# A fused attention and feed-forward kernel: the attention steps of two batches in another order, with empty steps, and a padded fifth chunk of keys

## The chip, the cores and the metric

The kernel runs on one core of a Trainium2 chip. The metric is the device time of one execution in microseconds; three runs of the kernel before gave a median of 1037.28 us (1033.76 to 1042.06).

## The reference

Causal attention over 4 batches of 8 heads, 576 positions and 64 columns per head, with a bias from running sums of `s`, then two feed-forward networks over the 2304 tokens:

```python
scores = scale * q @ k.T                    # per batch and head, 576 x 576
cum = cumsum(maximum(s, 0)); bias = -(cum[:, None] - cum[None, :])
scores = where(causal, -1e9, scores + minimum(bias, 0))
attn = softmax(scores) @ v                  # heads side by side: x is 2304 x 512
x = ((x @ w_a) * (x @ w_b)) @ w_out         # 512 -> 1536 -> 512
h = x @ w_in                                # 512 -> 2048
out = (maximum(h, 0) + alpha * minimum(h, 0)) @ w_out2   # 2048 -> 512
```

The weights arrive as 64-bit floats and are decoded on the chip.

## The kernel before

The tokens are cut into five blocks, four of 512 and one of 256. For each block `ffn` runs both networks. Every product is made of three TensorE multiplications of 512 columns (L997 to L999, L1106 to L1108): operands are split into a high and a low part (`xh`, `xl`, `wh`, `wl`, `gh`, `gl`), and low times low is left out. The weights are decoded in the first block, kept in memory as `w_d`, and loaded again as `raw` for each further block.

A batch has 576 rows, so its attention is done in two pieces: rows 0 to 511, four row blocks of 128 (r = 0 to 3), and the last 64 rows (r = 4), for which two heads share one tile. Attention of block 0's rows runs first, alone. The rest is cut into steps that stand between the multiplications of `ffn`: while the network of block n runs, the attention that block n + 1 needs is done, for rows 0 to 511 of batch a = n + 1 and the last 64 rows of batch b = n. There are four pairs of heads (i = 0 to 3), and for each pair these steps:

- `loads`: keys and queries (`kq`), values (`vb`), running sums (`cb`). `kq` has three buffers, `vb` four.
- `both` and `biases`: bias and causal mask of one or two row blocks are written to tiles `z`. `z` of r = 4 has one buffer.
- `s01`, `s23`, `s4`: scores of r = 0 and 1, of r = 2 or 3, and of r = 4 (L472, L647) go into two PSUM banks, which all attention steps share. `soften` then makes the probabilities: minimum, exponential, sum and scaling on VectorE, ScalarE and GpSimd.
- `turn`, `t4`: the probabilities are transposed by TensorE. Only batches below `TURN` = 2 do it so. From there on (`turned`) VectorE transposes within 32 x 32 squares into `zt`, which goes through memory (`zd<-zt`, then `pt<-zd` for r = 0 to 3 or `pb<-zd` for r = 4) to bring the squares into place. `pb` has one buffer, which `av_b` gives back.
- `two_av`: `av_b` (L766, or L774 in batches below `TURN`), then `av` (L707 or L714), probabilities times values; both wait until their probabilities are in place.

The function `attention` lists the steps of one block. Its first few (`lead`) are put among the steps of the block before, six from that list's end. The loop at the end of the kernel spreads the list over the `ffn`: a step is run when its share of 1 / 1.06 of the network's groups of three multiplications is reached, so the steps are evenly spaced, whatever they hold.

Nothing is ordered by the hardware or a compiler. While the program is written, the class `Order` keeps a clock for each engine and places VectorE's, ScalarE's, GpSimd's and SP's instructions by due times and by its own costs; `run.need` places what a step must have behind it. Each engine then serves its instructions strictly in the order placed. All loads and stores go through SP's one queue.

Of the kernel before, what the change touches and what calls it, by code (L numbers as in the profile page):

```python
# [18 lines left out]
P = 128  # L19
D = 64  # L20
# [33 lines left out]

SUMS_PE = 2

TURN = 2


FROM_WEIGHTS, AHEAD, FROM_LEAD, FROM_STEPS, STEPS = 2, 10, 3, 4, 3  # L60
# [132 lines left out]
def attention_two_moe_kernel(  # L193
# [10 lines left out]
    nc = tc.nc  # L204
# [8 lines left out]
    QA = 4 * P  # L213
    QB = S - QA
# [32 lines left out]
    SEEN = 100  # L247
# [28 lines left out]
    def scale(o, i, s0, s1):  # L276
        n = size(o)
        eng = yield Either(pool=115 + 1.09 * n, dve2=70 + 0.52 * n), SEEN
        (nc.gpsimd if eng == "pool" else nc.vector).tensor_scalar(
            o, i, s0, s1, op0=ALU.mult, op1=ALU.mult  # L280
        )

    def dma(o, i):
        yield {"sp": 480}, 700
        nc.sync.dma_start(o, i)
        yield {"dma": prod(o.shape) / 90}, 900
# [84 lines left out]
    pb_t, scores = {}, []  # L371
# [5 lines left out]
    def slot():  # L377

        ring.append(ring.pop(0))
        if ring[-1] in reader:  # L380
            run.need(reader[ring[-1]])
        return ring[-1]

    def read_by(i, gen):
        reader[i] = run.spawn(gen)
        return reader[i]

    def load_v(b, hp, u):
        c0 = 2 * hp * D
        got = []  # L390

        def chain():
            yield of_vb
            vr = raw.tile([P, 5, 2 * D], F32, name="vb", tag="vb", bufs=VB)
            got.append(vr)
            if b + u >= TURN:
                keys = v[b, 0:QA, c0:c0 + 2 * D].rearrange("(c j k) d -> j k c d", j=4, k=32)
                if u:
                    yield {"pool": 240}, SEEN
                    nc.gpsimd.memset(vr[:, 4, :], 0.0)  # L400
                for j in range(4):
                    yield from dma(vr[j::4, 0:4, :], keys[j])
                    if u and j < 2:
                        k0 = QA + 32 * j
                        yield from dma(vr[j::4, 4, :], v[b, k0:k0 + 32, c0:c0 + 2 * D])
                return
            yield from dma(
                vr[:, 0:4, :], v[b, 0:QA, c0:c0 + 2 * D].rearrange("(c p) d -> p c d", p=P)
            )
            if u:  # L410
                yield from dma(vr[0:QB, 4, :], v[b, QA:S, c0:c0 + 2 * D])

        v_t[b, hp, u] = got, run.spawn(chain(), slack=SL_QK)
# [72 lines left out]
    def biases(b, h, rs):  # L486
# [10 lines left out]
        def chain():  # L497
# [5 lines left out]
            c = 0  # L503
            if r == 4 and b + 1 >= TURN:
                yield {"pool": 180}, SEEN
# [40 lines left out]
    def turned(b, h, rs, z):  # L546

        yield of_zt
        n = z.shape[1] // P
        zt = work.tile([P, 4 * n * 32], F32, name="zt", tag="zt", bufs=ZT)  # L550
        zd = dram.tile([4, P, n * 32], F32, name="zd", tag=f"zd{n}", bufs=8)
        yield from dve(
            n * P, 1.04, nc.vector.transpose, zt.rearrange("p (j t n) -> p j t n", j=4, n=32),
            z.rearrange("p (t j n) -> p j t n", j=4, n=32),
        )
        run.give(of_z[rs[0]], run.t)
        yield from dma(
            zd.rearrange("i (k j) m -> (i k) (j m)", j=4), zt
        )
        run.give(of_zt, run.t)  # L560
        if rs[0] == 4:
            yield of_pb
            pb_t[h] = raw.tile([P, 5 * P], F32, name="pb", tag="pb")
            o = pb_t[h].rearrange("p (i m) -> p i m", i=4)
        else:
            s0 = rs[0] * (rs[0] + 1) // 2 * 32
            o = pts[h % 4].rearrange("p (i m) -> p i m", i=4)[:, :, s0:s0 + n * 32]
        yield from dma(o, zd.rearrange("i p m -> p i m"))

    def soften(b, h, rs, srcs, *banks_read):  # L570
# [14 lines left out]
        def rest():  # L585
# [10 lines left out]
            for i, p in enumerate(parts):  # L596
                yield from scale(p, p, sm[:, i:i + 1], 1.0)
            if b + (rs[0] == 4) >= TURN:
                e_t[b, h, rs[0]] = run.spawn(turned(b, h, rs, z), run.t)
# [54 lines left out]
    def probabilities(b, h, r):  # L654
        first = z_t[b, h, r][1]
        run.need(first)
        z, rest = z_t.pop((b, h, r))
        run.need(rest)
        return z
# [32 lines left out]
    def av(b, hp, blk):  # L692

        turned = b >= TURN
        if turned:
# [30 lines left out]
    def t4(b, hp, j):  # L726

        if j == 0:
            z_t[b, hp, 4] = probabilities(b, hp, 4)
        z = z_t[b, hp, 4]  # L730
        k, n = (QB, P) if j else (P, QA)
        at = slot()
        tp = banks[at][0:k, 0:n]
        for c in range(n // P):
            k0 = j * QA + c * P
            nc.tensor.transpose(tp[:, c * P:(c + 1) * P], z[:, k0:k0 + k], ident)
        run.pe(n / P * 107)
        if j:
            z_t.pop((b, hp, 4))
            run.give(of_z[4])  # L740

        def chain():
            if j == 0:
                yield of_pb
                pb_t[hp] = raw.tile([P, 5 * P], F32, name="pb", tag="pb")
            o = j * QA
            yield from copy(pb_t[hp][0:k, o:o + n], tp, 1.04)

        e_t[b, hp, 4 + j] = read_by(at, chain())

    def av_b(b, hp, blk):

        turned = b + 1 >= TURN
        if turned:
            settle((b, hp, 4))
        else:
            run.need(*(e_t.pop((b, hp, 4 + j)) for j in range(2)))
        got, ready = v_t.pop((b, hp, 1))
        run.need(ready)
        pb = pb_t.pop(hp)  # L760
        at = slot()
        pv = banks[at][:, 0:QB]
        for c in range(5 if turned else 0):
            for j in range(2):
                p = pb.rearrange("p (i t n) -> p i t n", i=4, n=32)
                nc.tensor.matmul(  # L766
                    pv[64 * j:64 * j + 64], got[0][:, c, j * D:(j + 1) * D],
                    p[:, 2 * j:2 * j + 2, c, :], start=c == 0, stop=c == 4,
                )
        for c in range(0 if turned else 5):  # L770
            for j in range(2):
                k = QB if c == 4 else P
                o = c * P + j * QB
                nc.tensor.matmul(  # L774
                    pv[64 * j:64 * j + 64], got[0][0:k, c, j * D:(j + 1) * D], pb[0:k, o:o + QB],
                    start=c == 0, stop=c == 4,
                )
        run.pe(5 * 107)
        run.give(of_vb)
        run.give(of_pb)  # L780
        x_done[blk].append(read_by(at, finish(pv, b * S + QA, QB, hp, blk)))
# [6 lines left out]
    HP = H // 2  # L788
# [46 lines left out]
    def attention(blk):  # L835

        b, a = blk - 1, blk
        has_a = a < B
        steps = []

        def add(f, pair, *args):
            if 0 <= pair < HP:
                steps.append((f, args))

        def loads(i):
            if has_a:
                load_kq(a, i, 0)
                if a >= SUMS_PE:
                    for j in range(2):
                        load_sums(a, 2 * i + j, 0)  # L850
                load_v(a, i, 0)
            load_kq(b, i, 1)
            load_sums(b, i, 1)
            load_v(b, i, 1)

        lead = [(loads, (0,))]
        if has_a:
            lead.append((both, (a, 0, (0, 1))))
        for i in range(HP + 1):
            j = i - 1  # L860

            def turns(c):
                for k in range(2 if a < TURN else 0):
                    add(turn, j, a, 2 * j + k, c)

            def last(p, k):
                if blk < TURN:
                    add(t4, p, b, p, k)

            if has_a:  # L870
                add(s01, i, a, i)
                add(both, i, a, i, (2,))
                turns(0)
                add(both, i, a, i, (3,))
                add(s23, i, a, i, 2)
                last(j, 0)
                turns(1)
                last(j, 1)
                add(s23, i, a, i, 3)
                add(biases, i, b, i, (4,))  # L880
                add(loads, i + 1, i + 1)
                turns(2)
                add(both, i + 1, a, i + 1, (0, 1))
                add(two_av, j, a, b, j, blk)
                add(s4, i, b, i)
            else:
                add(biases, i, b, i, (4,))
                add(loads, i + 1, i + 1)
                add(s4, i, b, i)
                last(i, 0)  # L890
                last(i, 1)
                add(av_b, i - (blk >= TURN), b, i - (blk >= TURN), blk)
        return lead, steps
# [230 lines left out]
    for blk in range(NB):  # L1124
# [5 lines left out]
        steps = plan[blk][1]  # L1130
# [76 lines left out]
```

## Time and profile before

| | before |
|---|---|
| median of three runs | 1037.28 us |
| profiled execution | 1038.65 us |
| its span on the core | 1036.9 us |
| TensorE busy | 1004.5 us (97%) |
| VectorE busy | 712.4 us (69%) |
| ScalarE busy | 541.7 us (52%) |
| GpSimd busy | 214.9 us (21%) |
| mean granted TensorE clock | 0.990 |

Times are microseconds from the start of the span. PE is TensorE, DVE VectorE, ACT ScalarE, POOL GpSimd, SPq SP's issue of a DMA. The attention that runs alone ends at about 56 us; the five network blocks end at about 287, 515, 740, 935 and 1035 us. A granted clock of 1.00 is the upper level (2.4 GHz), 0.50 the lower (1.2 GHz); a mean between them says that a stretch had both. A matmul's duration includes its way through the array, so neighbours overlap; pace is read from the starts.

### The profile page before, as it was taken

How to read it: one execution, taken by the hardware profiler on the slowest of the kernel's cores; microseconds unless marked ns; L12 is line 12 of the kernel's file. 1: busy time of each engine (PE TensorE's matmuls, PEld its weight loads, DVE VectorE, ACT ScalarE, POOL GpSimd, SP SyncE). 2: the span in 40 equal slices, each digit the busy share in tenths (PEclk: the TensorE clock that was granted, in tenths of full speed). 3: DMA queues.
4: the chain of work that ended last, by engine and by line, in shares of the span. 5: the costliest groups of instructions: out<-in, count | busy, mean ns of one | idle time of the engine just before them, and what ended most of it. 6: DMA issues, size and time to landing. Idle time of an engine off the chain costs nothing.

```text
span 1036.9 us, 16084 instructions
## 1 busy us (share of the span) xinstructions
PE 1004.5 (97%) x5385; PEld 807.2 (78%) x5385; DVE 712.4 (69%) x1693; ACT 541.7 (52%) x1124; POOL 214.9 (21%) x279
## 2 busy tenths in 40 slices
PE   6999999999999999999799999997999999999998
PEld 5577787777677787877678787876888888889997
DVE  6998998998866657677366859674444465545685
ACT  5876666666653446444254435452433344446564
POOL 2131211211111224232021214241100012210032
PEclk9999999999999999999899999998999999999999
DMA  7687968567857674875267575765335524227551
GB/s 199 192 268 258 296 236 287 177 211 249 275 169 195 203 206 153 225 194 183 71 201 227 176 209 174 191 193 164 127 99 164 175 70 147 95 74 250 184 178 39
DMA packets 128866, 191.53 MB, mean 185 GB/s; under 512 B 26576, under 2 KB 62416, under 8 KB 128784
## 3 DMA queue, kind: packets, MB, share of 16 engines
q1 hardware_dynamic: 128784, 190.51, 59.6%
q8 instruction: 42, 0.69, 0.3%
q14 instruction: 40, 0.33, 0.1%
HBM read 153.44 MB, written 37.04 MB: 184 GB/s over the span
## 4 chain that ended last, share of the span: by engine, by line
PE 70%; DMA 2%; DVE 1%; issue 1%; ACT 1%; SPq 0%; ACTq 0%; DVEq 0%
PE bank L997 16%; PE bank L998 16%; PE bank L999 16%; PE bank L1106 5%; PE bank L1107 5%; PE bank L1108 5%; PE bank L472 2%; PE bank L707 2%; DMA kq<-in_kq_a_dram 1%; PE bank L766 1%; PE bank L647 1%; ACT z L254 0%; DMA pb<-zd 0%; DVE wl L274 0%; DMA vb<-in_v_dram 0%
## 5 line engine op out<-in xcount | busy, mean ns | idle before, releaser
L997 PE MATMUL bank<-xh,wh 128*128 128x512 f32 (+1 forms) x800 | 303.5, 379 | 1.3 <-ACT wh L262 1.1
L999 PE MATMUL bank<-xh,wl 128*128 128x512 f32 (+1 forms) x800 | 296.0, 370 | 1.3 <-POOL wl L274 1.3
L998 PE MATMUL bank<-xl,wh 128*128 128x512 f32 (+1 forms) x800 | 295.5, 369 | 0.0
L262 ACT ACTIVATE wh<-raw 128x512 fp32r<-128x512 f32 x265 | 165.9, 627 | 113.0 <-PE bank L998 63.8
L274 DVE TENSOR_TENSOR wl<-raw,wh 128x512 fp32r<-128x512 f32 x200 | 139.6, 699 | 112.4 <-ACT wh L262 107.6
L997 PEld LDWEIGHTS bank<-xh,wh 128*128 128x128 f32 x800 | 151.2, 189 | 42.9 <-issue 13.4
L999 PEld LDWEIGHTS bank<-xh,wl 128*128 128x128 f32 x800 | 151.3, 189 | 28.2 <-POOL wl L274 2.2
L998 PEld LDWEIGHTS bank<-xl,wh 128*128 128x128 f32 x800 | 151.5, 189 | 24.3
L274 POOL TENSOR_TENSOR wl<-raw,wh 128x512 fp32r<-128x512 f32 x72 | 94.1, 1307 | 322.8 <-ACT wh L262 288.9
L262 ACT ACTIVATE gh<-g 128x512 fp32r<-128x512 f32 (+1 forms) x140 | 82.2, 587 | 66.3 <-DVE g L268 57.7
L274 DVE TENSOR_TENSOR gl<-g,gh 128x512 fp32r<-128x512 f32 (+1 forms) x125 | 87.9, 704 | 41.3 <-ACT gh L262 39.1
L1106 PE MATMUL bank<-wh,gh 128*128 128x512 f32 x288 | 115.3, 401 | 0.4 <-ACT wh L262 0.4
L1107 PE MATMUL bank<-wl,gh 128*128 128x512 f32 x288 | 112.6, 391 | 0.2 <-DVE wl L274 0.2
L1108 PE MATMUL bank<-wh,gl 128*128 128x512 f32 x288 | 112.4, 390 | 0.0
L254 ACT ACTIVATE z<-z,mn 128x128 f32<-128x128 f32 (+4 forms) x144 | 83.0, 579 | 49.5 <-DVE mn L268 49.4
L268 DVE SCALAR_TENSOR_TENSOR w<-raw,w 128x512 int32<-128x512 int32 x136 | 92.5, 699 | 0.1
L997 PE MATMUL bank<-gh,wh 128*128 128x512 f32 (+1 forms) x240 | 90.4, 377 | 0.0
L998 PE MATMUL bank<-gl,wh 128*128 128x512 f32 (+1 forms) x240 | 88.7, 369 | 0.3 <-DVE gl L274 0.2
L999 PE MATMUL bank<-gh,wl 128*128 128x512 f32 (+1 forms) x240 | 88.6, 369 | 0.0
L254 ACT ACTIVATE m<-bank 128x512 f32<-128x512 f32 (+1 forms) x80 | 44.1, 551 | 69.8 <-PE bank L999 69.6
L262 ACT ACTIVATE a_sb<-bank 128x512 f32<-128x512 f32 (+1 forms) x60 | 33.1, 552 | 76.6 <-PE bank L999 75.7
L1106 PEld LDWEIGHTS bank<-wh,gh 128*128 128x128 f32 x288 | 54.2, 188 | 13.8 <-issue 2.5
(83 smaller groups left out, 1321.8 us busy)
## 6 DMA issues: line engine op xcount, KB each, us to landing
raw<-w_d SPq DMA_DIRECT2D x136, 512.0 KB, 4.4
raw<-in_w_dram SPq DMA_DIRECT2D x68, 512.0 KB, 4.6
w_d<-w SPq DMA_DIRECT2D x68, 256.0 KB, 3.1
kq<-in_kq_a_dram SPq DMA_DIRECT2D x32, 256.0 KB, 5.7
zd<-zt SPq DMA_DIRECT2D x32, 192.0 KB, 1.9
pt<-zd SPq DMA_DIRECT2D x32, 192.0 KB, 2.9
kq<-in_kq_b_dram SPq DMA_DIRECT2D x16, 352.0 KB, 7.0
vb<-in_v_dram SPq DMA_DIRECT2D x80, 64.0 KB, 3.9
```

Of the source, the lines that this page charges most:

```text
L254: nc.scalar.activation(o, i, func, **k)
L262: nc.scalar.activation(o, i, AF.Copy)
L268: f(*args, **k)
L274: (nc.gpsimd if eng == "pool" else nc.vector).tensor_tensor(o, i0, i1, op=ALU.subtract)
L472: nc.tensor.matmul(dst[j], got[0][o, QA + r * P:QA + n], got[0][o, 0:n], start=b >= SUMS_PE, stop=True)
L707: nc.tensor.matmul(pv[64 * j:64 * j + 64, r * P:(r + 1) * P], got[0][:, c, j * D:(j + 1) * D], p[:, :, r * (r + 1) // 2 + c, :], start=c = ...
L997: nc.tensor.matmul(o, wh, ih, start=first, stop=False)
L998: nc.tensor.matmul(o, wh, il, start=False, stop=False)
L999: nc.tensor.matmul(o, wl, ih, start=False, stop=last)
L1106: nc.tensor.matmul(acc[t], gh[:, c], wh, start=first, stop=False)
L1107: nc.tensor.matmul(acc[t], gh[:, c], wl, start=False, stop=False)
L1108: nc.tensor.matmul(acc[t], gl[:, c], wh, start=False, stop=last)
```

## The change

For batches a >= `TURN`, which are the attention steps in the second and the third network block, the steps of a pair stand in another order. Before: `s01`, `both` (r = 2), `both` (r = 3), `s23` (2), `s23` (3), `biases`, `loads` of the next pair, `both` (0, 1) of the next pair, `two_av` of the pair before, `s4`. Now: `s4`, `s01`, `loads` of the next pair, `both` (2), `s23` (2), `both` (3), `two_av` of the pair before, `s23` (3), `biases` and `both` (0, 1) of the next pair. The first `biases` moves to the lead, which is run in the block before. Ahead of the last `two_av` five empty steps (`SPACE`) are put. The lists of these two blocks hold 45 and 43 steps with the next lead, instead of 40 and 39.

Besides, for the batch below `TURN` whose last 64 rows are done in the first block, the fifth chunk of keys (64 rows) is padded to 128: GpSimd sets the other 64 rows of `vb` and of `pb` to zero, and the two multiplications of that chunk run over 128 rows.

```diff
--- before.py
+++ after.py
@@ -54,7 +54,7 @@
 
 SUMS_PE = 2
 
-TURN = 2
+TURN, SPACE = 2, 5
 
 
 FROM_WEIGHTS, AHEAD, FROM_LEAD, FROM_STEPS, STEPS = 2, 10, 3, 4, 3
@@ -408,6 +408,8 @@
                 vr[:, 0:4, :], v[b, 0:QA, c0:c0 + 2 * D].rearrange("(c p) d -> p c d", p=P)
             )
             if u:
+                yield {"pool": 240}, SEEN
+                nc.gpsimd.memset(vr[QB:P, 4, :], 0.0)
                 yield from dma(vr[0:QB, 4, :], v[b, QA:S, c0:c0 + 2 * D])
 
         v_t[b, hp, u] = got, run.spawn(chain(), slack=SL_QK)
@@ -743,6 +745,8 @@
             if j == 0:
                 yield of_pb
                 pb_t[hp] = raw.tile([P, 5 * P], F32, name="pb", tag="pb")
+                yield {"pool": 240}, SEEN
+                nc.gpsimd.memset(pb_t[hp][QB:P, QA:5 * P], 0.0)
             o = j * QA
             yield from copy(pb_t[hp][0:k, o:o + n], tp, 1.04)
 
@@ -769,10 +773,9 @@
                 )
         for c in range(0 if turned else 5):
             for j in range(2):
-                k = QB if c == 4 else P
                 o = c * P + j * QB
                 nc.tensor.matmul(
-                    pv[64 * j:64 * j + 64], got[0][0:k, c, j * D:(j + 1) * D], pb[0:k, o:o + QB],
+                    pv[64 * j:64 * j + 64], got[0][:, c, j * D:(j + 1) * D], pb[:, o:o + QB],
                     start=c == 0, stop=c == 4,
                 )
         run.pe(5 * 107)
@@ -856,6 +859,8 @@
         lead = [(loads, (0,))]
         if has_a:
             lead.append((both, (a, 0, (0, 1))))
+            if a >= TURN:
+                lead.append((biases, (b, 0, (4,))))
         for i in range(HP + 1):
             j = i - 1
 
@@ -867,7 +872,20 @@
                 if blk < TURN:
                     add(t4, p, b, p, k)
 
-            if has_a:
+            if has_a and a >= TURN:
+                add(s4, i, b, i)
+                add(s01, i, a, i)
+                add(loads, i + 1, i + 1)
+                add(both, i, a, i, (2,))
+                add(s23, i, a, i, 2)
+                add(both, i, a, i, (3,))
+                if i == HP:
+                    steps.extend([(lambda: None, ())] * SPACE)
+                add(two_av, j, a, b, j, blk)
+                add(s23, i, a, i, 3)
+                add(biases, i + 1, b, i + 1, (4,))
+                add(both, i + 1, a, i + 1, (0, 1))
+            elif has_a:
                 add(s01, i, a, i)
                 add(both, i, a, i, (2,))
                 turns(0)
```

The end of the second block's attention on TensorE. Names: `kq` scores, `pb`, `vb` and `pt` as above; the other lines are the network's. Before, from the last pair's `s23` (3) to the last `two_av`:

```order
L472 MATMUL bank_95<-kq 128x512
L472 MATMUL bank_96<-kq 128x512
...
L766 MATMUL bank_95<-pb,vb 64x64 x10
...
L647 MATMUL bank_95<-kq 128x288
L647 MATMUL bank_96<-kq 128x288
L1106 MATMUL bank_99<-wh,gh 128x512
...
L766 MATMUL bank_95<-pb,vb 64x64 x10
```

Between the `kq` rows of 288 columns and the last `av_b` stand 21 network multiplications. The same place now:

```order
L649 MATMUL bank_95<-kq 128x288
L649 MATMUL bank_96<-kq 128x288
...
L770 MATMUL bank_95<-pb,vb 64x64 x10
...
L474 MATMUL bank_95<-kq 128x512
L474 MATMUL bank_96<-kq 128x512
L1015 MATMUL bank_97<-xh_104,wh 128x512
...
L770 MATMUL bank_95<-pb,vb 64x64 x10
```

Now the scores of 288 columns stand in front of that pair's other scores, 255 network multiplications before the last `av_b`, and those of 512 columns are the last, 153 before it (231 and 126 in the third block); before it was 21 and 78 (21 and 81 in the third).

The queue of SP at the loads of the second pair in the second block. `cb` are running sums, `raw` weights. Before:

```order
L285 DMA zd<-zt 128x512 x2
L285 DMA pt_109<-zd 128x4x128
L285 DMA kq<-in_kq_a_dram 64x1024
L285 DMA cb_3588<-cum_d 128x512
L285 DMA cb_3589<-cum_d 128x512
L285 DMA kq<-in_kq_b_dram 128x704
L285 DMA cb_3592<-cum_d 64x576
L285 DMA pt_110<-zd 128x4x128
L285 DMA raw<-w_d 128x2x512
L285 DMA kq<-in_kq_a_dram 64x1024
```

And now:

```order
L285 DMA zd<-zt 128x640
L285 DMA raw<-w_d 128x2x512
L285 DMA pb<-zd 128x4x160
L285 DMA kq<-in_kq_a_dram 64x1024
L285 DMA cb_3401<-cum_d 128x512
L285 DMA kq<-in_kq_b_dram 128x704
L285 DMA cb_3404<-cum_d 64x576
L285 DMA zd<-zt 128x384 x2
L285 DMA raw<-w_d 128x2x512
L285 DMA kq<-in_kq_a_dram 64x1024
```

The keys stood behind row block 3 (`zt` of 512 columns) of the first pair; now they stand around row blocks 0 and 1 (384 columns), which are done long before.

## Rows read from the trace of the kernel before

**Rows 1.** busy by stretch: length, PE PEld DVE ACT POOL (instructions), granted clock, DMA share, GB/s
```profile
72.00:270.00 198.00, 195.56 (x986) 150.46 (x985) 177.86 (x393) 127.19 (x255) 37.99 (x39) 1.00 0.74 246
...
285.00:485.00 200.00, 198.17 (x1005) 155.62 (x1005) 135.36 (x340) 96.70 (x205) 55.86 (x80) 0.99 0.67 192
485.00:505.00 20.00, 13.65 (x96) 11.58 (x95) 6.31 (x16) 3.49 (x9) 0.00 (x0) 0.83 0.48 158
...
710.00:732.00 22.00, 15.58 (x110) 13.06 (x109) 8.03 (x21) 5.75 (x13) 1.29 (x1) 0.84 0.34 111
```

**Rows 2.** waits of TensorE, 275 to 745 us: who, for whom, us, times, longest
```profile
PE bank L766 <- DMA pb<-zd: 6.4, 1, 6.4
PE bank L766 <- issue: 6.4, 1, 6.4
PE bank L472 <- DMA kq<-in_kq_a_dram: 1.6, 1, 1.6
PE bank L997 <- DVE g L268: 0.2, 1, 0.2
```

**Rows 3.** TensorE in order of time, 484 to 506 us: start, us, operation
```profile
486.94 1.13 PE L647 MATMUL bank<-kq 128*128 128x288 f32 x4
...
490.67 0.39 PE L997 MATMUL bank<-xh,wh 128*128 128x512 f32 x1
...
492.49 0.39 PE L999 MATMUL bank<-xh,wl 128*128 128x512 f32 x1
...
504.76 0.51 PE L997 MATMUL bank<-xh,wh 128*128 128x512 f32 x1
```

**Rows 4.** TensorE in order of time, 709 to 731 us
```profile
717.06 0.39 PE L999 MATMUL bank<-xh,wl 128*128 128x512 f32 x1
...
728.08 0.51 PE L997 MATMUL bank<-xh,wh 128*128 128x512 f32 x1
```

**Rows 5.** TensorE in order of time, 427 to 433 us
```profile
428.33 0.39 PE L1108 MATMUL bank<-wh,gl 128*128 128x512 f32 x1
428.65 0.80 PE L766 MATMUL bank<-pb,vb 128*64 128x64 f32 x20
429.28 2.36 PE L707 MATMUL bank<-pt,vb 128*64 128x128 f32 x40
431.57 0.50 PE L1106 MATMUL bank<-wh,gh 128*128 128x512 f32 x1
```

**Rows 6.** all engines but TensorE in order of time, 484 to 506 us
```profile
493.01 0.84 DVE L268 STREAM_TRANSPOSE zt<-z 128x640 f32<-128x640 f32 x1
...
496.06 0.36 SPq L285 DMA_DIRECT2D pb<-zd  x1
```

**Rows 7.** TensorE in order of time, 690 to 696 us
```profile
693.56 1.13 PE L472 MATMUL bank<-kq 64*128 64x512 f32 x4
```

**Rows 8.** SP's queue in order of time, 690 to 735 us
```profile
701.07 4.11 SPq L285 DMA_DIRECT2D pt<-zd  x2
```

**Rows 9.** the DMA issues: number, KB each, median us to landing
```profile
pt<-zd SPq DMA_DIRECT2D x16, 256.0 KB, 4.0
```

**Rows 10.** TensorE in order of time, 322 to 345 and 500 to 560 us
```profile
334.19 0.39 PE L999 MATMUL bank<-xh,wl 128*128 128x512 f32 x1
...
340.94 0.40 PE L999 MATMUL bank<-xh,wl 128*128 128x512 f32 x1
...
519.67 0.39 PE L999 MATMUL bank<-xh,wl 128*128 128x512 f32 x1
...
521.18 0.39 PE L998 MATMUL bank<-xl,wh 128*128 128x512 f32 x1
```

**Rows 11.** TensorE in order of time, 272 to 279 us
```profile
274.21 0.95 PE L774 MATMUL bank<-pb,vb 128*64 128x64 f32 x20
275.08 2.38 PE L714 MATMUL bank<-pt,vb 128*64 128x512 f32 x16
```

**Rows 12.** groups by line with their shapes kept apart, memsets on `vb`
```profile
L400 POOL MEMSET vb<- 128x128 f32 x12 | 2.5, 205 | 12.3 <-PE bank L707 12.0
```

## The prediction

> **What bounds the kernel now.** I began with the busy time by stretch [rows 1]. In the first network block (72 to 270 us) TensorE is busy 195.56 of 198 us while VectorE is busy 177.86; in the second (285 to 485) it is busy 198.17 of 200. TensorE sets the time nearly everywhere, so a change of order can only win where TensorE stands still or runs at the lower of its two clock levels. Two short stretches do not look like the rest: 485 to 505 has 13.65 us of work in 20 at a mean granted clock of 0.83, and 710 to 732 has 15.58 in 22 at 0.84.
>
> The second view, the waits of TensorE between 275 and 745 us [rows 2], names them: two waits of 6.4 us, both at L766, the first multiplication of `av_b`, and one of 1.6 us at L472, a score multiplication whose keys had not landed. Everything else in those 470 us is 0.2 us.
>
> The third view is TensorE's order of time at these places. Multiplications of 512 columns follow each other at (492.49 - 490.67) / 8 = 0.2275 us [rows 3]. The last one before the first wait starts at 492.49, and the first network multiplication behind the values at 504.76 [rows 3]. The second wait reads 717.06 to 728.08 [rows 4]. The same pair of steps without a wait takes 431.57 - 428.33 = 3.24 us [rows 5]. So the places cost 12.27 - 3.24 = **9.03 us** and 11.02 - 3.24 = **7.78 us**. That is more than 6.4 each, since the work right after a wait runs at the lower clock level, as the means of 0.83 and 0.84 say.
>
> Why L766 waits is read on the other engines [rows 6]: the last pair's probabilities of row block 4 are transposed on VectorE at 493.01, and their way through memory ends with the load of `pb`, issued at 496.06. The step that starts this chain (`s4`, L647 at 486.94 [rows 3]) is followed by `two_av`, which reads its end, after 21 network multiplications: 4.8 us of cover for a chain of about 12.
>
> **The change, part by part.**
>
> *The last `two_av`.* In the changed order `s4` of the last pair stands 255 network multiplications before the last `two_av` in the second block and 231 in the third, at 0.2275 us that is 58 and 52 us of cover. The chain of 12 us is hidden with room, so this wait goes. What is late next is row block 3, now the last step in front (`s23` with r = 3), with 153 and 126 multiplications behind it: 34.8 and 28.7 us. The same chain now: L472 with 512 columns at 693.56, the second of its two `pt` loads issued by 705.18, landing 4.0 us later by the median [rows 7 to 9]: 15.6 us. It gets SP rows of the next batch's loads in front of it, which I bound by its own length again (31 us). In the second block that still fits; in the third, where the batch ahead has fewer loads, it need not. I take both waits as gone: **-16.8 us**.
>
> *The keys of the second pair.* `loads` moves from behind row block 3 to right behind `s01`. Before, TensorE waited for its last half: from 334.19 to 340.94 for the scores and up to the ninth multiplication behind them [rows 10], where the same piece takes (521.18 - 519.67) + 7 x 0.2275 = 3.10 us without a wait. That is 6.75 - 3.10 = **3.65 us**, more than twice the wait itself, again by the lower clock. Now about 139 multiplications (31 us) lie between `loads` and that `s01`, against some 60 (14 us) before, and `s4` gives its key buffer back before `loads` asks for one. I take -3.65; between 0 and that is the range.
>
> *The padding.* In the first block each `av_b` ends with two multiplications per head pair over 64 rows instead of 128. Its 20 multiplications take 275.08 - 274.21 = 0.87 us [rows 11], those of L766, all over 128 rows, 429.28 - 428.65 = 0.63 us [rows 5]. Four such steps: 4 x 0.24 = **-0.96 us**. The Trainium skill (TensorE: Matmul & The Clock Gate, Why this matters for your kernels) holds that a multiplication over few rows takes the same time as one over 128; by that the padding gives nothing and the sum is 1.0 us higher. The rows decide, since they compare the very same shapes but for the chunk.
>
> *What is added.* Eight memsets on GpSimd, 205 ns for a like one [rows 12], all in the first block, where VectorE is 90% busy; and the bias of row block 4 of the next batch is built at the end of that block rather than later. The four on `pb` stand ahead of the copy that frees a bank, the four on `vb` ahead of a small load. Nothing waits for them directly; the cover is that TensorE lost only 2.44 us in that block [rows 1]. The lower bound is 0. For the upper one I take all eight in full (1.6 us) and the present loss once more (2.4 us): 4 us. I take **+1.0**, near the lower end, because even VectorE at 90% cost TensorE so little. The Trainium skill (GPSIMD Engine Reference, 8. Key points) says that GpSimd shares its memory interfaces with VectorE and holds up some of its instructions. That rule speaks against the memsets; if each held VectorE for its whole length it would be 1.6 us by the row, inside the bound.
>
> *The empty steps.* Five steps that do nothing make the others come closer together: a block of 512 tokens has 12 x 36 + 16 x 24 = 816 network multiplications, so 816 / (1.06 x 45) = 17.1 multiplications per step in the second block, against 816 / (1.06 x 40) = 19.2. VectorE, 68% busy there (135.36 of 200 [rows 1]), gets the attention's share of its work in a shorter stretch, and more at the same total is still under the 90% of the first block. I cost that at nothing; if the cover is gone it is the 2.4 us of the first block, twice.
>
> Sum: -16.8 - 3.65 - 0.96 + 1.0 = **-20.4 us**. Against the profiled execution's own 1038.65 us that is 1018.2; the median of the three runs, 1037.28, is 1.4 us lower, which makes 1016.9. I forecast **1017 us**, with 1013 to 1022 as this case's own range: additions at nothing and the runs' scatter below their median (1033.76 against 1037.28) below, additions at their bound and the wait for keys half left above.
>
> **The rivals.**
>
> *A. The wait only changes its name.* The last `two_av` waits for `pt` of row block 3 instead of `pb`. For it: that step is now the nearest in front, and the next batch's loads share its queue. Against it: 28.7 us of cover for 15.6. It would show in the third block first; one of the two places returned in full is 1017 + 8 = 1025 us, both 1034.
>
> *B. Slower: masks late.* `both` for row block 2 now stands one step (17 multiplications, 3.9 us) before the scores that read it, and the bias of row block 4 two steps before `s4`; they were two and four steps. If bias and mask came later than that, VectorE, which serves in order, would hold both score banks and, behind it, the weights' low parts. It decides from the point where they take longer than the 3.9 us and the 33 multiplications (7.5 us) until the banks are next written, 11 us in all. Each place priced as the wait for keys (3.65 us), the eight of one kind are +29, 1046 us, and those of both kinds +58, 1075 us. Against it: TensorE waited for no mask in any of the 470 us [rows 2], and the old order had places of two steps.
>
> *C. The first block pays.* Its order shifts throughout (one step more at its end, and so all of them a little earlier), at 90% of VectorE. Were its loss to grow from 2.4 to some 8 to 14 us, the time is 1023 to 1029 us. Nothing in the rows asks for it beyond the high load.
>
> *D. The change does nothing*: the waits stay where they are and shrink elsewhere by nothing, 1037 us. The order excludes this for `pb`, whose chain now starts ten times earlier.
>
> **How the numbers follow.** Forecast 76 in 100; A 9, half of it with both places; B 5; C 8; D 2. Within 1% is 1026.9 to 1047.7 us, which is about what a measurement here can tell. Faster by over 1%: the forecast (0.76), A with one place (0.04), most of C (0.06): 0.86. Within 1%: A with both, the rest of C, D and half of B: 0.11. Slower by over 1%: the other half of B: 0.03. The range from 1009 to 1027 us takes the forecast with its bounds, A with one place and most of C, and leaves out about 14 in 100; its lower end allows for the scatter of the runs about their median.
>
> **What would show it.** In the profile of the changed kernel no wait at `av_b` of several microseconds, a granted clock of 1.00 in the stretches that held the two waits, no wait for `kq` in the second block, all 20 multiplications of the first block's `av_b` in 0.63 us, and a loss in the first block still of 2 to 4 us. A wait of several microseconds at L709 in the third block would make A right, score banks held by VectorE with GpSimd as releaser would make B right. The prediction is wrong if TensorE's idle time in the second and third blocks is not under 2 us.

## The result, and the profile after

The changed kernel takes 1021.5 us in the median of four runs (1020.95 to 1026.48), the kernel before 1037.6 (four runs, 1033.76 to 1042.06). The ratio is 0.985 with a 95% interval from 0.980 to 0.990: faster by 16 us, 1.0 to 2.0%. The profiled execution took 1020.95 us with a span of 1018.8, against 1038.65 and 1036.9.

Both traces are cut at the same four instructions: the first scores of row block 4, and the first network multiplication behind the last `two_av` of the first, second and third network block. The time ahead of the first cut is 61.38 us before and 59.35 after. The view is the busy time by stretch of the kernel before, with columns as in [rows 1]:

```profile
61.38:277.39 216.01, 212.80 (x1093) 163.15 (x1091) 195.45 (x440) 138.14 (x280) 40.66 (x41) 1.00 0.75 248
277.39:504.76 227.37, 219.19 (x1133) 173.26 (x1131) 148.38 (x367) 104.73 (x221) 57.87 (x81) 0.98 0.66 192
504.76:728.08 223.32, 216.90 (x1139) 171.88 (x1137) 147.06 (x364) 102.62 (x216) 53.72 (x76) 0.98 0.61 179
728.08:1036.90 308.82, 304.82 (x1697) 263.34 (x1695) 170.79 (x308) 150.30 (x282) 49.56 (x51) 1.00 0.41 134
```

And of the changed kernel:

```profile
59.35:280.34 220.99, 214.53 (x1092) 163.47 (x1090) 199.02 (x440) 140.83 (x283) 41.04 (x49) 0.99 0.75 243
280.34:494.57 214.23, 214.23 (x1132) 169.35 (x1131) 144.33 (x359) 105.00 (x220) 70.93 (x90) 1.00 0.68 203
494.57:710.06 215.49, 215.49 (x1138) 170.56 (x1136) 142.46 (x354) 106.81 (x222) 59.54 (x76) 1.00 0.62 185
710.06:1018.80 308.74, 304.78 (x1697) 263.38 (x1695) 170.97 (x308) 150.40 (x282) 49.55 (x51) 1.00 0.41 134
```

The second block lost 13.14 us and the third 7.83; TensorE is now busy in all of both, at a granted clock of 1.00. The stretch behind them is the same to 0.1 us. The first block took 4.98 us more, with TensorE idle in 6.46 of them instead of 3.21. The stretch ahead of it was 2.03 us shorter.

TensorE's order of time at the last `two_av` of the second and of the third block, which answers to [rows 3] and [rows 4]:

```profile
491.33 0.39 PE L1017 MATMUL bank<-xh,wl 128*128 128x512 f32 x1
491.65 0.80 PE L770 MATMUL bank<-pb,vb 128*64 128x64 f32 x20
492.29 2.36 PE L709 MATMUL bank<-pt,vb 128*64 128x128 f32 x40
494.57 0.50 PE L1015 MATMUL bank<-xh,wh 128*128 128x512 f32 x1
...
706.83 0.39 PE L1017 MATMUL bank<-xh,wl 128*128 128x512 f32 x1
...
710.06 0.50 PE L1015 MATMUL bank<-xh,wh 128*128 128x512 f32 x1
```

3.24 and 3.23 us, what [rows 5] showed for the pair without a wait. The waits of TensorE over the whole span (who, for whom, us, times, longest) hold no `av_b`, and nothing at all in the second and third block; behind them one of 0.2 us is left. The larger ones are in the first block or ahead of it:

```profile
PE bank L676 <- DVE z L279: 3.1, 2, 2.0
PE bank L1015 <- ACT wh L262: 2.5, 2, 1.8
PE bank L1015 <- ACT gh L262: 1.8, 1, 1.8
PE bank L474 <- DMA kq<-in_kq_a_dram: 1.8, 2, 1.0
```

The padded `av_b` of the first block, against [rows 11]: 278.09 - 277.45 = 0.64 us where it was 0.87.

```profile
277.45 0.80 PE L777 MATMUL bank<-pb,vb 128*64 128x64 f32 x20
278.09 2.33 PE L716 MATMUL bank<-pt,vb 128*64 128x512 f32 x16
```

### The profile page after: what moved, and what is told of

The parts are those of the page before. It is cut to its first block, busy times and chain, and to the rows that moved or that the text cites. A ratio compares the mean times of both kernels' runs of the same rounds, so it can differ in the third digit from the quotient of the medians.

```text
span 1018.8 us, 16095 instructions
## 1 busy us (share of the span) xinstructions
PE 997.8 (98%) x5385; PEld 800.3 (79%) x5385; DVE 707.5 (69%) x1675; ACT 548.4 (54%) x1132; POOL 234.6 (23%) x297
## 4 chain that ended last, share of the span: by engine, by line
PE 87%; DMA 5%; DVE 5%; ACT 1%; issue 1%; SPq 0%; POOL 0%; ACTq 0%; POOLq 0%; DVEq 0%
PE bank L1015 20%; PE bank L1017 19%; PE bank L1016 19%; PE bank L1124 6%; PE bank L1125 6%; PE bank L1126 6%; PE bank L474 3%; DMA w_d<-w 2%; DVE w L268 2%; PE bank L709 2%; PE bank L649 1%; PE bank L716 1%; DMA kq<-in_kq_a_dram 1%; PE bank L676 1%; DMA raw<-in_w_dram 1%
## 5 line engine op out<-in xcount | busy, mean ns | idle before, releaser
L262 ACT ACTIVATE wh<-raw 128x512 fp32r<-128x512 f32 x268 | 167.9, 627 | 103.1 <-PE bank L1016 62.9
L274 DVE TENSOR_TENSOR wl<-raw,wh 128x512 fp32r<-128x512 f32 x186 | 129.8, 699 | 105.6 <-ACT wh L262 96.8
L274 POOL TENSOR_TENSOR wl<-raw,wh 128x512 fp32r<-128x512 f32 x86 | 112.6, 1309 | 359.4 <-ACT wh L262 304.0
L274 DVE TENSOR_TENSOR gl<-g,gh 128x512 fp32r<-128x512 f32 (+1 forms) x120 | 83.3, 694 | 42.3 <-ACT gh L262 40.5
L279 DVE TENSOR_SCALAR m<-m,alpha_sb 128x512 f32<-128x512 f32 (+1 forms) x70 | 32.0, 457 | 53.9 <-ACT m L254 52.8
```

The costliest lines, as they stand in the source:

```text
L262: nc.scalar.activation(o, i, AF.Copy)
L274: (nc.gpsimd if eng == "pool" else nc.vector).tensor_tensor(o, i0, i1, op=ALU.subtract)
L279: (nc.gpsimd if eng == "pool" else nc.vector).tensor_scalar(o, i, s0, s1, op0=ALU.mult, op1=ALU.mult)
```

## The experiments

Each was timed beside the kernel before on one chip, where that took 1038.7 us (e1 to e4), 1038.0 (e5 to e8), 1039.4 (e9 to e11) and 1039.9 (e12) in the median; the ratio is to it, with its interval, and medians of different chips are not to be set against each other. "First" to "third" are the stretches between the cuts above, from the profiled execution. "Late" is the part of "first" from its 81st network multiplication on; "list" is the length of the first block's list of steps against the kernel before.

| kernel | list | first | late | second | third | span | median | ratio |
|---|---|---|---|---|---|---|---|---|
| before |  | 216.0 | 195.7 | 227.4 | 223.3 | 1036.9 | 1037.6 | |
| changed | +1 | 221.0 | 199.9 | 214.2 | 215.5 | 1018.8 | 1021.5 | 0.985 (0.980 to 0.990) |
| e1 order only | +1 | 221.5 | 200.2 | 214.2 | 215.6 | 1021.7 | 1023.7 | 0.985 (0.981 to 0.989) |
| e2 padding only | as before | 213.7 | 193.4 | 224.3 | 223.2 | 1030.0 | 1035.1 | 0.996 (0.994 to 0.998) |
| e3 no empty steps | +1 | 220.0 | 199.4 | 220.1 | 224.0 | 1036.7 | 1036.9 | 0.998 (0.996 to 1.000) |
| e4 empty steps only | as before | 215.9 | 194.8 | 216.2 | 217.8 | 1020.8 | 1026.3 | 0.989 (0.983 to 0.994) |
| e5 bias at home | as before | 215.8 | 194.8 | 214.2 | 215.9 | 1017.8 | 1018.4 | 0.981 (0.978 to 0.984) |
| e6 empty lead step | +1 | 222.7 | 198.1 | 215.4 | 215.1 | 1022.0 | 1022.9 | 0.985 (0.982 to 0.989) |
| e7 old order, loads early | as before | 214.9 | 194.6 | 214.2 | 216.3 | 1017.1 | 1018.8 | 0.981 (0.978 to 0.984) |
| e8 two empty steps | +1 | 218.2 | 198.2 | 214.5 | 215.5 | 1016.7 | 1019.5 | 0.982 (0.978 to 0.986) |
| e9 one lead step | as before | 222.3 | 199.2 | 214.2 | 215.5 | 1023.2 | 1019.1 | 0.982 (0.979 to 0.984) |
| e10 changed again | +1 | 219.1 | 199.2 | 214.2 | 215.5 | 1020.3 | 1021.9 | 0.983 (0.981 to 0.986) |
| e11 e7 with two steps | as before | 220.3 | 196.9 | 214.3 | 215.5 | 1018.5 | 1016.7 | 0.979 (0.977 to 0.981) |
| e12 before, longer list | +1 | 222.5 | 199.6 | 223.0 | 224.3 | 1040.9 | 1042.3 | 1.002 (1.000 to 1.005) |

**e1, the order without the padding.** The six lines of the padding undone, as in the kernel before:

```diff
-                yield {"pool": 240}, SEEN
-                nc.gpsimd.memset(vr[QB:P, 4, :], 0.0)
...
+                k = QB if c == 4 else P
```

> The change without its padding: the fifth chunk is again two multiplications over 64 rows, and the eight memsets are gone. Theory O (the moved biases and the longer list of steps cost the first block its 5 us): the first block takes 221 us from its first row-block-4 scores to the end of its last values as in the changed kernel, plus 1.0 for the slower multiplications; total 1021 to 1023. Theory P (the padding's memsets cost it): 216 us there, total 1016 to 1018. Blocks two and three as in the changed kernel, 214 and 215 us.

221.5 us in the first block: the memsets are not what it pays for. The second and third blocks are those of the changed kernel, so the padding has no part in their gain. From the 81st multiplication on the first block took 200.2 us, no less than with the memsets.

**e2, the padding without the order.** The same edits put into the kernel before.

> The padding alone, steps in the old order. Theory O: no cost, 1 us less for the multiplications: 1036 to 1038, the first block 215 to 216 us. Theory P: the first block takes 220 to 221 us, total 1041 to 1043. In both the two waits of 6.4 us at the last values and the one for the keys stay.

Theory O's side, and more: the first block took 213.7 us and the median fell by 0.44% (0.23 to 0.64%), 2 to 7 us, where 1 was forecast. The two waits at `av_b` stayed. The wait for keys, which both theories had staying, did not: it was 0.3 us instead of 1.6, with `loads` where they were, and the second block was 3.1 us shorter than in the kernel before.

**e3, the changed kernel with no empty steps.**

```diff
-TURN, SPACE = 2, 5
+TURN, SPACE = 2, 0
```

> The changed kernel with no empty steps. Theory R (the last values then wait for row block 3, 18 to 21 multiplications or 4 to 5 us behind its scores, against a chain of 15.6 us): two waits of 9 to 11 us with 1.5 to 2.5 us each of lower clock behind them, total 1043 to 1048. Theory S (moving the scores of the last 64 rows to the front is enough): no wait, 1021.

Theory R in kind, not in size. TensorE's order of time at the end of the second block, from the scores of row block 3 on:

```profile
487.49 1.13 PE L474 MATMUL bank<-kq 64*128 64x512 f32 x4
...
493.55 0.80 PE L770 MATMUL bank<-pb,vb 128*64 128x64 f32 x20
494.18 1.48 PE L709 MATMUL bank<-pt,vb 128*64 128x128 f32 x24
498.96 0.43 PE L709 MATMUL bank<-pt,vb 128*64 128x128 f32 x2 [3.31 <-DMA pt<-zd]
500.49 1.97 PE L709 MATMUL bank<-pt,vb 128*64 128x128 f32 x14 [1.09 <-DMA pt<-zd]
502.39 0.79 PE L1015 MATMUL bank<-xh,wh 128*128 128x512 f32 x1
502.98 0.63 PE L1016 MATMUL bank<-xl,wh 128*128 128x512 f32 x1
503.41 0.63 PE L1017 MATMUL bank<-xh,wl 128*128 128x512 f32 x1
```

`av_b` no longer waits, but the values do, for row block 3: the wait has changed its name. It is 4.4 us and not 9 to 11, because 24 of the 40 multiplications need only row blocks 0 to 2 and run first, and the chain from 487.49 to 500.49 is 13.0 us rather than 15.6. The pace behind it is 0.43 us for a multiplication instead of 0.2275. Together the two blocks take 14.3 us more than in the changed kernel, and the whole gain of the change is gone.

**e4, five empty steps alone, the old order.**

```diff
+                if a >= TURN and i == HP:
+                    steps.extend([(lambda: None, ())] * SPACE)
                 add(two_av, j, a, b, j, blk)
```

> The old order with five empty steps ahead of the last values in the same two blocks, no padding. Theory R (what counts is the distance to the last values): 123 to 135 multiplications (28 to 31 us) now cover the chain of 12 us, both waits go, 16.8 us less; the wait for keys (3.65 us) stays; total 1020 to 1022, first block 216 us. Theory S (the order is needed): waits of several microseconds stay, 1030 or more.

Theory R: no wait at `av_b`, blocks of 216.2 and 217.8 us, 16.7 us less than before in the two together (11.2 and 5.5, where 9.03 and 7.78 had been priced for the two waits). The median, 1026.3, is above the forecast; two of its four runs took 1030 and 1032 us. TensorE's waits behind 282 us, but for one of 0.2 us, are these; the first line is 1.5 us in the second block and 0.7 in the third, the other is in the third:

```profile
PE bank L472 <- DMA kq<-in_kq_a_dram: 2.2, 2, 1.5
PE bank L1000 <- POOL gl L274: 0.9, 1, 0.9
```

**e5, the first bias in its own block.** Out of the lead, and that block's first `s4` behind its `s01`:

```diff
-            if a >= TURN:
-                lead.append((biases, (b, 0, (4,))))
...
+                if i == 0:
+                    add(biases, i, b, i, (4,))
+                    add(s01, i, a, i)
+                    add(s4, i, b, i)
```

> The changed kernel, but the first bias of row block 4 is built in its own block again, and that block's first s4 stands behind its s01; the first block's list of steps is as in the kernel before. If the reordering's cost there (5 us) comes from what it adds to that list: first block 213 to 215 us (216.0 less some 1.2 to 2.3 for the padding), blocks two and three 214 to 216, total 1013 to 1016. If it comes from anything else, such as the program being another one: 219 to 221 there, total 1021.

215.8 us in the first block and a median of 1018.4, both somewhat above the forecast, which speaks for the list as the cause.

**e6, an empty step in the lead** in the place of the bias, else as e5.

```diff
-                lead.append((biases, (b, 0, (4,))))
+                lead.append((lambda: None, ()))
```

> As the one with the bias at home, but an empty step stands in the lead where the bias was, so that the first block's list is as long as in the changed kernel and without its work. If the bias's own work at the crowded end costs the 5 us: first block 213 to 215 us, total 1013 to 1016. If the other spacing of all its steps does: 219 to 221 us, total 1020 to 1022.

222.7 us without any of the bias's work in the first block: it is not that work. This kernel differs from e5 by the empty step alone and ran beside it: its four runs (1022.39 to 1023.83) all lie above e5's six (1016.47 to 1020.51), with medians 4.6 us apart. TensorE's order of time shows where the longer list is paid:

```profile
177.08 0.50 PE L1020 MATMUL bank<-gh,wh 128*128 128x512 f32 x1 [1.37 <-ACT gh L262]
260.83 0.50 PE L1020 MATMUL bank<-xh,wh 128*128 128x512 f32 x1 [1.55 <-ACT wh L262]
```

These are the 429th and the 721st network multiplication of the first block. At both, the changed kernel, e10, e3 and e8 wait for ScalarE too, 1.0 to 1.8 and 1.3 to 2.7 us; e2, e5, e7 and e11, with the padding and the old length, wait at neither. Against those, the five profiles with the longer list take 3.8 to 6.6 us more over the two places.

**e7, the old order with `loads` moved.** Padding and five empty steps as well.

```diff
                 add(s01, i, a, i)
+                if a >= TURN:
+                    add(loads, i + 1, i + 1)
```

> The old order with the padding, five empty steps, and of the reordering only this: loads of the next pair stand behind s01. If the reordering's gain in blocks two and three is the wait for keys alone: no wait for keys in the second block, 214 to 215 and 215 to 216 us there, first block 213 to 215, total 1013 to 1017. If the place of s4 and the biases matters as well: blocks of 216 to 218 us as with the empty steps alone, total 1018 to 1021.

214.2 and 216.3 us (215.5 in e11): what the new order gives the two blocks beyond the empty steps is the early `loads`. In those blocks TensorE waits 0.3 us in all.

**e8, two empty steps.**

```diff
-TURN, SPACE = 2, 5
+TURN, SPACE = 2, 2
```

> The changed kernel with two empty steps instead of five. Without any, the last values waited 3.3 and 1.1 us for row block 3 in either block; a step is 17 to 20 multiplications or about 4 us. If distance alone counts, two steps (8 us) cover it: no wait, 214 and 216 us, total 1020 to 1023. If the next batch's loads that fall between push the chain back, waits of 1 to 4 us stay and the total is 1024 to 1032.

No wait, and blocks as with five. Two steps cover it: 54 and 60 network multiplications now stand between the scores of row block 3 and the last `two_av`, 12.3 and 13.7 us at full pace, where e3 had 21 and 18.

**e9, the lead's `both` and `biases` as one step**, so that the list is as long as before and the bias still moved.

```diff
-            lead.append((both, (a, 0, (0, 1))))
+            def first():
+                both(a, 0, (0, 1))
+                if a >= TURN:
+                    biases(b, 0, (4,))
+
+            lead.append((first, ()))
```

> The changed kernel, with the lead's two last entries made one step that does both: the bias is still built at the end of the first block, but its list of steps is as long as in the kernel before. If the spacing of the steps costs the first block its 3 to 6 us (lists one longer: 218 to 223 us in five profiles; as before: 214 to 216 in five): 214 to 216 us there, total 1016 to 1019. If the bias's work costs it: 218 to 222, total 1020 to 1023.

Undecided by its numbers. The median, 1019.1, is on the side of the spacing; the profiled execution, at 1024.98 us the slowest of its five, has a first block of 222.3. It has neither of the two waits of the longer list; it waits 3.2 us for `wh` at the 769th multiplication, where the other profiles wait 1.5 or less. Whether the bias's work has to do with that, one profile does not show.

**e10, the changed kernel once more.**

> The changed kernel once more, beside the others on one chip: 1020 to 1023, first block 218 to 222 us, the two others 214 and 216. If its first block is 216 or less here, what was put down to the list of steps is scatter.

1021.9 and 219.1, as expected.

**e11, e7 with two empty steps.**

> The old order with the padding, loads behind s01, and two empty steps instead of five. If two steps are enough here too (8 us and the 4 us that were there, for a chain of 12): no wait at the last values, 1016 to 1020 as with five. If not: waits of 1 to 3 us twice, 1021 to 1027.

The lowest median, 1016.7 us, 2.1% under the kernel before (1.9 to 2.3%), and under the changed kernel's 1021.9 beside it on the same chip. Its first block, however, shows what single profiles of that block are worth. Up to the second block it has the same instructions in the same order as e7. The busy time of the first block in e7, and in e11, up to the 81st network multiplication and from it:

```profile
62.94:83.22 20.28, 20.22 (x101) 15.94 (x99) 19.50 (x52) 12.26 (x27) 5.05 (x6) 1.00 0.83 258
83.22:277.86 194.64, 191.74 (x992) 146.20 (x991) 177.90 (x391) 127.81 (x255) 32.31 (x38) 1.00 0.76 247
```

```profile
59.60:83.06 23.46, 22.23 (x103) 17.28 (x101) 19.09 (x53) 12.93 (x28) 5.00 (x6) 0.93 0.78 242
83.06:279.92 196.86, 193.01 (x992) 147.44 (x991) 177.88 (x391) 126.77 (x254) 31.90 (x38) 0.99 0.75 245
```

5.4 us apart for one program. 3.2 of them are in the first part: e11 comes to the block 3.3 us sooner, waits 1.13 us for keys at 65.58, and is at the 81st multiplication when e7 is. The other 2.2 are scatter behind it.

**e12, the kernel before with one empty step in the lead.**

```diff
             lead.append((both, (a, 0, (0, 1))))
+            if a >= TURN:
+                lead.append((lambda: None, ()))
```

> The kernel before with one empty step in the lead of the second block, so that the first block's list is one longer and nothing else is added there. If the other spacing of the first block's steps costs 3 us or more in the median: 1041 to 1044, first block 218 us or more. If the first block's differences are scatter between runs: 1037 to 1040, within 0.15% of the kernel before on the same chip.

2.3 us slower beside the kernel before, with an interval from nothing to 4.7. The median of 1042.3 looks like the first reading, but the kernel before took 1039.9 on that chip. The profile narrows it: from the 81st multiplication on the block took 199.6 us, where the kernel before and e4, the same program there but for the empty step, took 195.7 and 194.8; it has one wait for `wh` of 4.1 us (266.32, the 733rd multiplication) that those two do not have, and that e1, also longer and without the padding, has with 3.9 us.

## Why the prediction was right, and where it was not

The forecast was 20.4 us less; the runs give 16.1. What the second and third block were to give came in nearly in full; the first block took back more than the sum had for it.

- *What bounds the kernel, and the two waits (-16.8).* Right in place and size: both pairs of steps now take what [rows 5] gave, the third block lost 7.83 us where 7.78 had been priced, and e4 removes both waits with nothing but distance. That e4's sum, 16.7, meets the 16.8 is in part luck: its second block also has a cheaper wait for keys, its third two small waits of its own. The price taken, the whole excess and not the 6.4 us of the wait, was the right one: e3 shows the same lower pace behind its shorter waits.
- *The keys (-3.65).* Right for the profile that it was read from: the second block lost 13.14 us, 9.03 for its wait and 4.1 more, and with `loads` early (the changed kernel, e7, e11) TensorE does not wait for these keys. But the price was that of one run. In e4 a wait of 1.54 us at the same place (330.82 to 335.92, read as [rows 10]) cost 5.10 - 3.10 = 2.00 us, because the granted clock stayed at 1.00 behind it, and in e2 and e12, with `loads` where they had been, the wait was 0.3 us and none at all. That 4.1 meets 3.65 is the luck of that profile; against e4, moving `loads` gives 1.9 and 1.6 us. The stretches of 5 us in the kernel before and in e4:

```profile
336.00:341.00 5.00, 4.40 (x15) 3.33 (x16) 2.40 (x11) 1.11 (x4) 0.00 (x0) 0.66 0.88 257
333.00:338.00 5.00, 4.84 (x24) 3.85 (x25) 3.58 (x13) 2.39 (x9) 0.00 (x0) 1.00 0.39 111
```

- *The padding (-0.96).* Right for the steps themselves, 0.23 us each, and 0.06 more in the `av` behind each. The rule that I weighed against it, that of the Trainium skill (TensorE: Matmul & The Clock Gate, Why this matters for your kernels), that a multiplication over few rows takes as long as a full one, nearly holds (228 and 243 ns, rows below), and it does not speak of what the group as a whole takes. The trace shows where that goes: in the last group of the kernel before, pairs of multiplications start about 0.05 us apart, but 0.15 us pass at the change from 128 rows to 64 (274.67 to 274.82) and 0.15 again at the change back (274.93 to 275.08); padded, 0.05 pass at both places. The Trainium skill (TensorEngine Tiling (Array Packing), Key Properties) says that TensorE drains when the tiling mode changes; these gaps agree with it. e2's whole gain is larger than these steps; in its profile 3.1 us of it are in the second block, where the wait for keys was shorter.
- *What is added (+1.0).* This is the step that was mis-sized, and its cost lay in something that the sum had at nothing: the list of the first block's steps that is one longer, which only rival C names. The memsets are not it (e1, e2; seven of the eight are in that block, one stands ahead of it), nor the bias's work (e6). e6 against e5 is 4.6 us in the median for the one step, and the profiles with it show waits for ScalarE that none of the old length has. From the 81st multiplication on, the changed kernel's program took 198.2 to 199.9 us in four profiles (with e10, e3, e8) and that of the kernel before 195.7 and 194.8 (with e4): 2.5 to 5.1 us more, with the padding's gain inside, where the two terms together had been forecast at nothing. Why ScalarE is late at just these places in the shifted order stays open. TensorE's idle time in the block, 6.46 us, is outside the 2 to 4 that were to show the forecast right. That the time still fell into the range is in part luck: with the padding's 1.2 us put back the additions cost 3.7 to 6.3 us, and their bound was 4.
- *The empty steps (0).* Right that they cost nothing in the blocks that hold them, and under-read in weight: without them (e3) the change gains nothing, and with them alone (e4) the two blocks gain 16.7 of 21 us. Five are more than are needed (e8, e11).
- *The rivals.* A is what e3 shows; with the empty steps there was no such wait. B did not occur: TensorE waits for nothing in blocks two and three. C was right in place, and a little too high in price: it had the block's loss growing by 6 to 12 us, and the block grew by 5.0 in the first profile and by 2 to 4 in the three others of the same program (e10, e3, e8).

The multiplications of the first block's `av_b` in the kernel before, over 128 and over 64 rows, in the view of groups with their shapes kept apart (after the bar: busy us, mean ns of one):

```profile
L774 PE MATMUL bank<-pb,vb 128*64 128x64 f32 x64 | 2.7, 228 | 0.0
...
L774 PE MATMUL bank<-pb,vb 64*64 64x64 f32 x16 | 1.3, 243 | 0.0
```

Two in ten of these are 64 rows deep. Taken by itself each is hardly slower; what a group loses stands between them, at the two changes.

The two waits of the longer list as they stand in the changed kernel, in TensorE's order of time:

```profile
171.11 0.39 PE L1017 MATMUL bank<-gh,wl 128*128 128x512 f32 x1
173.31 0.50 PE L1015 MATMUL bank<-gh,wh 128*128 128x512 f32 x1 [1.81 <-ACT gh L262]
...
174.38 0.39 PE L1017 MATMUL bank<-gh,wl 128*128 128x512 f32 x1
...
255.27 0.39 PE L1126 MATMUL bank<-wh,gl 128*128 128x512 f32 x1
257.44 0.52 PE L1015 MATMUL bank<-xh,wh 128*128 128x512 f32 x1 [1.79 <-ACT wh L262]
...
258.25 0.80 PE L1017 MATMUL bank<-xh,wl 128*128 128x512 f32 x1
258.85 0.63 PE L1015 MATMUL bank<-xh,wh 128*128 128x512 f32 x1
...
261.44 0.39 PE L1017 MATMUL bank<-xh,wl 128*128 128x512 f32 x1
```

The same two pieces take 0.68 and 2.38 us in e7, where neither waits; here they take 3.27 and 6.17. So the first wait costs 2.6 us and the second, as long, 3.8: from 258.25 the multiplications follow at 0.43 to 0.60 us, about twice the usual pitch, until about 261.

## What to carry to other kernels

Where an in-order engine must not stand still, price a wait from the last multiplication at full pace to the first one at full pace again, not by the idle time that the waits' view gives, and in more than one run: the same wait for keys cost 3.65 us in one kernel's profile and 2.00 in another's. To remove it, count the cover in instructions between the step that starts a chain and the step that reads its end, for every chain that ends there: moving one chain forward alone only hands the wait to the next. A stage that waits in many small places varies from run to run; compare it over several runs, piece by piece from the same instruction to the same instruction, and do not read its cost from one trace.

## What the runs showed of the hardware

A wait of 1 to 2 us may or may not be followed by the lower clock. Behind the two waits of the changed kernel's first block the granted clock was 1.00 and 0.66:

```profile
173.00:178.00 5.00, 4.47 (x40) 2.60 (x42) 4.71 (x9) 3.18 (x7) 1.36 (x2) 1.00 0.85 260
257.00:262.00 5.00, 4.55 (x14) 3.33 (x15) 4.54 (x8) 2.13 (x4) 0.00 (x0) 0.66 1.05 291
```

In e8, the same program up to there, the second of them (1.69 us, at 255.80) was followed by 1.00 as well.

The same program can run its first microseconds at two speeds. The changed kernel's two profiled executions, between 10 and 30 us, the first and then e10:

```profile
10.00:30.00 20.00, 17.97 (x139) 13.49 (x137) 17.25 (x96) 16.41 (x55) 6.24 (x13) 1.00 0.83 250
```

```profile
10.00:30.00 20.00, 18.05 (x117) 13.80 (x116) 14.14 (x83) 14.43 (x47) 4.99 (x11) 0.91 0.84 236
```

TensorE was busy as long in both, but did 139 multiplications at a granted clock of 1.00 and 117 at 0.91. The first cut then came at 59.35 and 62.69 us. All fourteen profiles fall into these two kinds: five reach it at 59.4 to 60.1 us with a mean granted clock of 1.00 ahead of it, nine at 61.4 to 62.9 with 0.97. So the 2.03 us by which the changed kernel reached its first cut sooner are no gain of the change.
